# Which partial sums ScalarE copies out of PSUM, the order of six product chains, and the last store of a fused attention and FFN kernel

## Chip, core and metric

The kernel runs on one core of a Trainium2 chip. The metric is the time of one execution in microseconds (us) of device time. TensorE (PE) does the matmuls and loads their weights (PEld), VectorE (DVE) does elementwise work and scans, ScalarE (ACT) does copies and activations, GpSimd (POOL) masks, and SyncE (SP) issues every DMA.

## What is computed

A gated linear attention (batch 4, 8 heads, 768 steps, head size 48) is followed by a multiplicative feed-forward network on 3072 tokens of width 384:

```python
for t in range(S):
    state = f[:, :, t, :, None] * state + np.einsum('bhd,bhe->bhde', k[:, :, t], v[:, :, t])
    y[:, :, t] = np.einsum('bhd,bhde->bhe', q[:, :, t], state)
...
a = x @ w1
b = x @ w2
h = a * b @ w3
return (h @ w_out).astype(np.float32)
```

Everything is fp32. `w3 @ w_out` is folded into one 1024x384 matrix `wc` on the chip, so that the FFN is two "up" products (384 to 1024), their elementwise product, and one "down" product (1024 to 384).

## The kernel before, in words

The tokens go in six blocks of 512 (`ffn(n)`, n = 0 to 5). Attention runs in 24 units of 128 tokens and has ended by about 265 us; what follows is FFN work alone. Block 0 is computed plainly (`part`), blocks 1 and 2 by a seven-product scheme (`seven`), and blocks 3 to 5 by a bilinear scheme with 20 products in place of 24 (`many`). The change is in `many` and in `down`.

`many(g)` runs twice per block (g = 0, 1), so six times in all. It forms 20 products. Product (a, b) multiplies the a-th input (three token quarters by two halves, and sums of them, `X_SUMS`) by the b-th weight (twelve blocks of `w12`, and sums of them, `W_SUMS`), for `w1` and `w2` at once: two matmuls of 128x256 into the two halves of one PSUM bank of 128x512 (L1114). The products are arranged in six chains (`CHAINS`). A chain lives in one bank: its first product opens the bank, each later one adds to what is there, so that the bank holds a running sum. Twelve sums (`Y_SUMS`, L1158, VectorE) combine the running sums, and eight elementwise products (L1170, or L1174 with L1177 for the one that is a bank alone) give the result `ab`.

A running sum is read in one of two ways. If it is in the set `kept` (L1113 to L1116), ScalarE copies it to SBUF (`keep_`, L1135), and the next product of the chain waits for that copy, since it overwrites the bank by adding to it. If not, VectorE reads the bank itself in the sum (L1158). Before, only the last running sum of a chain can be read directly, so that no product waits for such a read. Twelve of the twenty are copied.

PSUM has eight banks. Four are tiles of one bank each (`f0` to `f3`). The other four are the halves of two tiles of two banks, `pa` and `py`, which attention uses whole; after attention, `bank()` (L369) hands out their halves one by one.

The order of all work is decided when the program is built: each step is put into `Plan` with an engine, an assumed cost, what it needs, a priority and the bank or temporary it takes, and `Plan.order` lists the steps by the earliest assumed start. Each engine then runs its instructions strictly in that order, and waits on semaphores for data of the others. Beside the FFN, ScalarE carries a check of the value range of the raw weights (`ranges`, L1513 to L1521): for each of 34 pieces, SP loads 512 KB into one of two buffers and ScalarE makes two passes over it, L1517 and L1521. These stand between the copies in ScalarE's order.

`down(i)` (twice per block) computes 2x128 output rows by seven groups of four matmuls of 128x192 (L863: m1, m6, m2, m7, m5, m4, m3), with copies by ScalarE (k1 at L1231, c11 at L1244) and sums by VectorE (u2 at L1237, u3 at L1250, c22 at L1261, c21 at L1267, c12 at L1275). c11 writes columns 0 to 191 of the upper rows, c12 columns 192 to 383. SP stores each 128 rows by one DMA of 192 KB (L1280).

In the names of the profile, the weights of product (a, b) show as the home of W sum b: `w` for b below 12, floor for b = 12, q for 15, 17, 25 and 26, k for 18, 19, 20 and 30, f for 21 and 22, bwd for 31, Q for 32, and K for 28 and 33.

Of the kernel before, what the change touches and what calls it, by code (L numbers as in the profile page):

```python
# [45 lines left out]
P = 128  # L46
# [5 lines left out]
DM = H * D  # L52
# [12 lines left out]
DH = DM // 2  # L65
# [25 lines left out]
W_LATE = 30  # L91
W_SINCE = 0.0
W_STEP = 0.0
CHAINS = [
    [(3, 0), (4, 4), (4, 23)],
    [(0, 13), (1, 6), (1, 26)],
    [(5, 8), (9, 25), (6, 17), (10, 31)],
    [(8, 28)],
    [(11, 14), (12, 22), (3, 19)],
    [(7, 10), (16, 21), (14, 12), (15, 32), (17, 30), (0, 33)],  # L100
]
X_SUMS = [
    (1, '+', 2, 0), (2, '+', 0, 1), (2, '+', 5, 2), (1, '+', 8, 3), (9, '+', 4, 4), (0, '+', 8, 5),
# [7 lines left out]
]  # L111
Y_SUMS = [
    (10, '+', 11), (7, '-', 20), (21, '-', 5), (4, '+', 14), (20, '-', 8), (24, '-', 18),
    (6, '+', 1), (13, '-', 16), (12, '+', 2), (28, '-', 15), (12, '-', 17), (30, '-', 9),
]
Y_ENDS = [22, 19, 23, 25, 26, 27, 29, 31]
NWT = 15
NXT = 11
FLOOR = 2.0**-60
# [141 lines left out]
def ranged(ctx, tc, q, k, f_logit, v, w1, w2, w3, w_out, out, ident, w12, wc, left):  # L261

    nc = tc.nc
# [70 lines left out]
    plan = Plan()  # L334
# [95 lines left out]
    def moves(n, size, rate, emit, deps, prio, late=0.0, since=0.0, lanes=("lane",)):  # L430


        for j in range(n):
            i = plan.add("SP", 0.45, (lambda: None) if j else emit, [d] if j else deps, prio - j * 1e-3, takes=lanes, lag=0.85, since=since)
            d = i
            t = plan.add("DMA", size / n / rate, lambda: None, [i], prio - j * 1e-3, lag=1.1 + late, frees=[i])
        return t
# [419 lines left out]
    stores, upq, downq, w_nodes, opened = [], [], [], [], []  # L857
# [10 lines left out]
    def ffn(n):  # L868
# [203 lines left out]
        def many_sums():  # L1072
            for k, (i, o, j, h) in enumerate(W_SUMS if not w_nodes else []):
                def emit(i=i, o=o, j=j, k=k):
                    nc.vector.tensor_tensor(w_view(4 * KM + k), w_view(i), w_view(j), op(o))
                w_nodes.append(plan.add("DVE", 0.69, emit, [over] + w_nodes[-1:], 100 * MANY + W_LATE + k, since=W_SINCE + W_STEP * k))
            old = [q[nm] for m in (n - 1, n - 2) for q in blk[m].get("seven", []) for nm in ("m5", "m6", "m7", "m4", "m3")]
# [8 lines left out]
        def many(g):  # L1086

            if ("X", 0) not in s:
                many_sums()
            n0 = 100 * n + 50 + 4 * g  # L1090
            np_ = sum(len(c) for c in CHAINS)
            uses = {}
            for i, _, j in Y_SUMS:
                for x in (i, j):
                    uses[x] = uses.get(x, 0) + 1
            task, bank_of, where_, hold, readers = {}, {}, {}, {}, {}
            ends_of = {}
            t = 0
            for c in CHAINS:
                ends_of[t + len(c) - 1] = True  # L1100
                t += len(c)
            kept = set()
            for i, _, j in Y_SUMS:
                direct = [x for x in (i, j) if x in ends_of and uses[x] == 1 and x not in Y_ENDS]
                kept |= {x for x in (i, j) if x < np_ and x not in direct[-1:]} if len(direct) < 2 else {min(direct)}
            begin = takes_ab(column(0, g), plan.add("PE", 0.0, lambda: None, x_task(0) + opened[-1:], n0))

            def product(t, c, first, a, b):
                def emit():
                    if first:  # L1110
                        banks[g, c] = bank()
                    for which in range(2):
                        lhs = up_weights(w12, which, b // 4, column(b % 4, g)) if b < 4 * KM else w_view(b)[:, which, g]  # L1113
                        nc.tensor.matmul(  # L1114
                            banks[g, c][:, which * TH : which * TH + TH], lhsT=lhs, rhs=x_node(a),
                            start=first and which == 0, stop=True, skip_group_check=True,  # L1116
                        )
                return emit

            banks = {}  # L1120
            t = 0
            for c, chain in enumerate(CHAINS):
                last = None
                for m, (a, b) in enumerate(chain):
                    deps = [begin] + x_task(a) + ([w_nodes[b - 4 * KM]] if b >= 4 * KM else []) + ([last] if m else opened[-1:])
                    task[t] = last = plan.add("PE", 0.86, product(t, c, m == 0, a, b), deps, n0 + 0.1 * c - 0.01 * m, takes=["f"] if m == 0 else [])
                    s["up"].append(last)
                    if m == 0:
                        opener = last
                        opened.append(last)  # L1130
                    bank_of[t] = (c, opener)
                    if t in kept:
                        def keep_(t=t, c=c):
                            where_[t] = temporary(plan.got)
                            nc.scalar.copy(where_[t], banks[g, c])  # L1135
                        last = plan.add("ACT", 0.57, keep_, [last], n0 - 200, takes=["t"], frees=[opener] if t in ends_of else [])
                        task[t] = hold[t] = last
                    t += 1
            left_ = dict(uses)
            for k, (i, o, j) in enumerate(Y_SUMS):  # L1140
                r = np_ + k
                deps = [task[i], task[j]]
                frees, mine = [], None
                for x in (i, j):
                    left_[x] -= 1
                    if x in hold and not left_[x] and x not in Y_ENDS:
                        deps += readers.get(x, [])
                        if mine is None:
                            mine = x
                        else:  # L1150
                            frees.append(hold[x])
                    elif x not in hold:
                        frees.append(bank_of[x][1])

                def emit(i=i, o=o, j=j, r=r, mine=mine):
                    x, y = (where_[v] if v in where_ else banks[g, bank_of[v][0]] for v in (i, j))
                    where_[r] = temporary(plan.got) if mine is None else where_[mine]
                    nc.vector.tensor_tensor(where_[r], x, y, op(o))  # L1158

                task[r] = plan.add("DVE", 0.69, emit, deps, n0 - 200, takes=["t"] if mine is None else [], frees=frees)  # L1160
                hold[r] = task[r] if mine is None else hold[mine]
                for x in (i, j):
                    readers.setdefault(x, []).append(task[r])
            for e, r in enumerate(Y_ENDS):
                def target(e=e):
                    return a_b(column(e % 4, g))[:, e // 4 * TH : e // 4 * TH + TH]

                if r in hold:
                    def emit(r=r, target=target):
                        nc.vector.tensor_tensor(target(), where_[r][:, 0:TH], where_[r][:, TH:TB], ALU.mult)  # L1170
                    done = plan.add("DVE", 0.43, emit, [task[r]] + readers.get(r, []), n0 - 200, frees=[hold[r]])
                else:
                    def half(r=r, target=target):
                        nc.scalar.copy(target(), banks[g, bank_of[r][0]][:, 0:TH])  # L1174
                    h = plan.add("ACT", 0.38, half, [task[r], begin], n0 - 200)
                    def emit(r=r, target=target):
                        nc.vector.tensor_tensor(target(), banks[g, bank_of[r][0]][:, TH:TB], target(), ALU.mult)  # L1177
                    done = plan.add("DVE", 0.43, emit, [h], n0 - 200, frees=[bank_of[r][1]])
                s["done"][g].append(done)
            s.setdefault("many", []).extend(task.values())  # L1180
# [13 lines left out]
        def down(i):  # L1194
            q = {}
            downq.append(q)
            final = n == NB - 1 and i == UB // 2 - 1
# [76 lines left out]
            def c12():  # L1274
                nc.vector.tensor_tensor(q["o1"][:, DH:DM], q["Z"], dns["u2"], ALU.add)  # L1275

            def store(half):
                def emit():
                    t0 = n * TB + (i + half * UB // 2) * P
                    nc.sync.dma_start(out[t0 : t0 + P], q["o1" if half == 0 else "o2"])  # L1280
                return emit

            n0 = 100 * n + 90 + i + 60 * (n > 1) + 30 * (n == NB - 2)
# [28 lines left out]
            pe("m3", m3, [q["c22"], q["S3"], q["m4"]] + ([judged] if final else []), -4)  # L1312
            dve("c12", 0.36, c12, [q["m3"], q["c11"]], frees=[q["m5"]])
            for half, deps in ((1, ("c21", "c22")), (0, ("c11", "c12"))):
                stores.append(moves(1, 197, 300, store(half), [q[nm] for nm in deps], -10))
            return q

        for i in range(UB // 2):
            q = down(i)
# [274 lines left out]
    first, last = {}, {}  # L1594
    for item in EARLY:
        if item in "ABCD":
            half, which = divmod("ABCD".index(item), 2)
            mine = pieces[which, half]
            first[item], last[item] = [j["deps"][0] for j in mine], mine
        else:  # L1600
            t = tk[int(item)]
# [389 lines left out]
```

## Time and profile before

| | us |
|---|---|
| median of 3 runs (465.94 to 467.49) | 466.26 |
| the profiled execution | 466.62 |
| its span | 464.9 |
| ScalarE busy, whole span | 206.8 |
| VectorE busy, whole span | 364.9 |
| first product of `many` starts on PE | 275.36 |
| end of the last instruction on VectorE (c12 of the last `down`) | 460.31 |

The profiled execution took 1.7 us more than its span, which runs from its first to its last instruction. Times in the text are from the span's start. A row of the timeline merges equal neighbours: "x4" at L1114 is one product, because each fp32 matmul is recorded as two. The length of a PE row includes the pipeline's depth, so that two rows that follow without a gap overlap; how far apart their starts are is what tells of a stall. The text in brackets at the end of a row is the idle time of the engine before it and the engine and line that ended it.

### The profile page before, as it was taken

The page shows a single profiled execution, that of the slowest core. Times are in us where ns is not written, and L with a number is a line of the kernel's source. Part 1 is how long each engine was busy: PE and PEld are TensorE (multiplying, and loading weights), DVE is VectorE, ACT ScalarE, POOL GpSimd, SP SyncE. Part 2 cuts the span into 40 slices and gives each one's busy share as a digit, 9 for nine tenths or more (in the row PEclk, how much of TensorE's full clock was granted, in tenths as well). Part 3 has the DMA queues.
Part 4 walks back from the last instruction along what each step waited for, and adds up shares of the span by engine and source line. Part 5 has one row for each costly group of instructions (what it writes and reads, how often), then busy time and mean ns, then how long its engine had stood idle before and what let it go on. Part 6 is the DMA issues. An engine that isn't in the chain of part 4 may idle for free.

```text
span 464.9 us, 11763 instructions
## 1 busy us (share of the span) xinstructions
PE 454.4 (98%) x4800; PEld 396.0 (85%) x4800; DVE 364.9 (78%) x657; ACT 206.8 (44%) x468; POOL 64.6 (14%) x90
## 2 busy tenths in 40 slices
PE   8989999999999999999999999999999999999995
PEld 7778886666899888889998889998899977889995
DVE  8988999999898998989973599894687366867451
ACT  4565344532224444443332456565764567642000
POOL 9330001121122332322331000000000000000000
PEclk9999999999999999999999999999999999999999
DMA  6899898733346664545423336534364433100111
GB/s 180 263 307 282 276 347 276 261 96 93 83 111 191 200 181 122 140 134 165 106 64 107 120 124 204 170 129 151 119 202 159 151 122 94 45 1 0 35 68 39
DMA packets 43165, 68.75 MB, mean 148 GB/s; under 512 B 5201, under 2 KB 28242, under 8 KB 42082
## 3 DMA queue, kind: packets, MB, share of 16 engines
q1 hardware_dynamic: 43106, 67.95, 47.5%
q8 instruction: 39, 0.64, 0.6%
q14 instruction: 20, 0.16, 0.1%
HBM read 58.88 MB, written 9.04 MB: 146 GB/s over the span
## 4 chain that ended last, share of the span: by engine, by line
PE 94%; POOL 2%; DVE 1%; issue 1%; ACT 0%; POOLq 0%; DVEq 0%
PE f L863 25%; PE f L959 14%; PE f L1114 12%; PE f L1446 9%; PE pa L1114 5%; PE py L1114 5%; PE py L863 5%; PE pa L863 3%; PE py L619 3%; PE pa L545 2%; PE pa L652 2%; PE f L559 2%; PE py L638 2%; PE pa L959 1%; POOL ab L403 1%; PE f L365 1%
## 5 line engine op out<-in xcount | busy, mean ns | idle before, releaser
L675 POOL TENSOR_SCALAR_AFFINE_SELECT A<-A 64x512 f32<-64x512 f32 (+1 forms) x46 | 43.4, 943 | 104.5 <-ACT A L669 102.3
L1446 PE MATMUL f<-place 128*128 128x384 f32 x128 | 42.7, 488 | 0.0
L863 PE MATMUL f<-xt,w 128*128 128x256 f32 x192 | 42.1, 380 | 0.0
L863 PEld LDWEIGHTS f<-xt,w 128*128 128x128 f32 x192 | 36.3, 190 | 5.0
L1446 PEld LDWEIGHTS f<-place 128*128 128x128 f32 x128 | 23.8, 190 | 15.3
L959 PE MATMUL f<-xt,w 128*128 128x256 f32 x132 | 34.2, 379 | 0.0
L863 PE MATMUL f<-place 128*128 128x192 f32 x184 | 33.9, 329 | 0.0
L514 DVE TENSOR_TENSOR_SCAN bwd<-gate,back 112x512 f32<-112x512 f32 x24 | 30.9, 1285 | 0.7
L492 DVE TENSOR_TENSOR_SCAN fwd<-gate,floor 112x512 f32<-112x512 f32 x24 | 30.5, 1271 | 1.1 <-ACT gate L484 0.2
L863 PEld LDWEIGHTS f<-place 128*128 128x128 f32 x184 | 30.1, 190 | 0.8 <-DVE place L1237 0.3
L959 PEld LDWEIGHTS f<-xt,w 128*128 128x128 f32 x132 | 24.8, 190 | 3.1
L1521 ACT ACTIVATE A<-A,back 128x512 f32<-128x512 f32 x34 | 26.6, 781 | 0.5
L811 ACT ACTIVATE ys<-py 112x512 f32<-112x512 f32 x22 | 13.1, 595 | 28.2 <-PE py L638 27.3
L1384 ACT ACTIVATE place<-place 128x512 f32<-128x512 uint32 (+2 forms) x24 | 21.1, 890 | 9.9 <-DMA place<-in_w_dram 7.6
L1517 ACT ACTIVATE A<-A 128x512 f32<-128x512 f32 x34 | 23.3, 685 | 4.0 <-DMA A<-in_w_dram 4.0
L863 PE MATMUL f<-wc,ab 128*128 128x192 f32 x128 | 23.4, 326 | 0.0
L959 PE MATMUL f<-place 128*128 128x256 f32 x84 | 22.4, 385 | 0.0
L775 POOL TENSOR_TENSOR G<-lasts,gate 112x4 f32<-112x4 f32 x20 | 10.7, 533 | 81.3 <-ACT lasts L497 50.0
L863 PEld LDWEIGHTS f<-wc,ab 128*128 128x128 f32 x128 | 21.3, 190 | 0.3
L484 ACT ACTIVATE gate<-f 112x512 f32<-112x512 f32 x22 | 13.9, 632 | 15.8 <-DMA f<-in_f_logit_dram 5.6
L619 PEld LDWEIGHTS py<-A,vt 64*64 64x64 f32 (+1 forms) x672 | 13.3, 127 | 7.3 <-issue 5.7
L619 PE MATMUL py<-A,vt 64*64 64x64 f32 (+1 forms) x672 | 18.1, 223 | 0.2
(343 smaller groups left out, 1041.5 us busy)
## 6 DMA issues: line engine op xcount, KB each, us to landing
A<-in_w_dram SPq DMA_DIRECT2D x28, 512.0 KB, 3.9
place<-in_w_dram SPq DMA_DIRECT2D x8, 1024.0 KB, 6.7
place<-in_w_dram SPq DMA_DIRECT2D x12, 512.0 KB, 7.5
out_dram<-o SPq DMA_DIRECT2D x24, 192.0 KB, 1.9
q<-in_q_dram SPq DMA_DIRECT2D x46, 96.0 KB, 2.9
vt<-in_v_dram SPq DMA_DIRECT2D x23, 192.0 KB, 3.2
k<-in_k_dram SPq DMA_DIRECT2D x44, 96.0 KB, 2.6
yt<-ys SPq DMA_DIRECT2D x44, 96.0 KB, 2.7
```

The costliest lines, as they stand in the source:

```text
L484: nc.scalar.activation(gate[u % 2][:, 0:NQ], fu, AF.Sigmoid)
L492: nc.vector.tensor_tensor_scan(s["P"], gate[u % 2][:, 0:NQ], floor, 0.0, ALU.mult, ALU.max)
L514: nc.vector.tensor_tensor_scan(s["R"][:, ::-1], gate[u % 2][:, NQ:0:-1], back[:, ::-1], 0.0, ALU.mult, ALU.max)
L619: done = nc.tensor.matmul(y_block(u, hp, par, half)[p0 : p0 + w], lhsT=s["v"][half * W : half * W + W, h * D : h * D + w], rhs=s["A"][half ...
L675: nc.gpsimd.affine_select(out=a, in_=a, pattern=pattern, compare_op=ALU.is_ge, fill=0.0, base=0, channel_multiplier=-1,)
L863: nc.tensor.matmul(out_, lhsT=lhs[i], rhs=rhs[i], start=start and i == 0, stop=i == len(lhs) - 1, skip_group_check=True,)
L959: nc.tensor.matmul(q[nm][:, which * TH : which * TH + TH], lhsT=lhs[i](which), rhs=rhs[i], start=start and which == 0 and i == 0, stop=i = ...
L1114: nc.tensor.matmul(banks[g, c][:, which * TH : which * TH + TH], lhsT=lhs, rhs=x_node(a), start=first and which == 0, stop=True, skip_grou ...
L1384: nc.scalar.activation(lo.bitcast(F32), lo, AF.Copy, bias=2.0, scale=2.0**-51)
L1446: nc.tensor.matmul(w3s["p", jc], lhsT=w3s[jc][:, kc * P : kc * P + P], rhs=wos[:, kc], start=(kc == 0), stop=(kc == KF - 1),)
L1517: return lambda: nc.scalar.activation(a, a, AF.Abs, accum_out=sums_[:, i : i + 1])
L1521: return lambda: nc.scalar.activation(a, a, AF.Sign, bias=small, accum_out=counts[:, i : i + 1])
```

## The change

```diff
+SLACK_M = 0.0
+DIRECT = 1
 CHAINS = [
     [(3, 0), (4, 4), (4, 23)],
+    [(5, 8), (9, 25), (6, 17), (10, 31)],
     [(0, 13), (1, 6), (1, 26)],
-    [(5, 8), (9, 25), (6, 17), (10, 31)],
+    [(7, 10), (16, 21), (14, 12), (15, 32), (17, 30), (0, 33)],
+    [(11, 14), (12, 22), (3, 19)],
     [(8, 28)],
-    [(11, 14), (12, 22), (3, 19)],
-    [(7, 10), (16, 21), (14, 12), (15, 32), (17, 30), (0, 33)],
 ]
...
-            for i, _, j in Y_SUMS:
-                direct = [x for x in (i, j) if x in ends_of and uses[x] == 1 and x not in Y_ENDS]
-                kept |= {x for x in (i, j) if x < np_ and x not in direct[-1:]} if len(direct) < 2 else {min(direct)}
+            latest = {i: i for i in range(np_)}
+            for k, (i, _, j) in enumerate(Y_SUMS):
+                late_, other = (i, j) if latest[i] > latest[j] else (j, i)
+                latest[np_ + k] = latest[late_]
+                alone = late_ < np_ and uses[late_] == 1 and late_ not in Y_ENDS and (late_ in ends_of or DIRECT)
+                kept |= {x for x in (i, j) if x < np_ and not (x == late_ and alone)}
...
-                    elif x not in hold:
+                    elif x not in hold and x in ends_of:
                         frees.append(bank_of[x][1])
...
                 task[r] = plan.add("DVE", 0.69, emit, deps, n0 - 200, takes=["t"] if mine is None else [], frees=frees)
+                for x in (i, j):
+                    if x < np_ and x not in hold and x not in ends_of:
+                        made[x + 1]["deps"].append(task[r])
...
-            def store(half):
+            def store(half, c0=0, c1=DM):
                 def emit():
                     t0 = n * TB + (i + half * UB // 2) * P
-                    nc.sync.dma_start(out[t0 : t0 + P], q["o1" if half == 0 else "o2"])
+                    nc.sync.dma_start(out[t0 : t0 + P, c0:c1], q["o1" if half == 0 else "o2"][:, c0:c1])
...
             for half, deps in ((1, ("c21", "c22")), (0, ("c11", "c12"))):
+                if final and half == 0:
+                    stores.append(moves(1, 98, 300, store(0, 0, DH), [q["c11"]], -10))
+                    stores.append(moves(1, 98, 300, store(0, DH, DM), [q["c12"]], -10))
+                    continue
```

`Y_SUMS` and `Y_ENDS` are renumbered to the new order of the products; the sums are the same twelve. The new rule for `kept` looks at each sum of two running sums and takes the one whose product comes later in the list: if it is used once, VectorE reads it from the bank, whether or not its chain goes on; the other one, and any that is used more than once, is copied. Where the chain goes on, its next product waits for the VectorE sum in place of a copy (`made[x + 1]`).

Read directly before: (8,28), (1,26), (3,19), (4,23) and (10,31), each the end of its chain. Read directly after: (8,28) and (3,19), which end their chains, and (5,8) and (7,10), which open theirs. So (5,8) and (7,10) lose their copy, and (4,23), (1,26) and (10,31) gain one: thirteen copies per call of `many` in place of twelve. The product (9,25) now waits for the sum (5,8)+(4,4), and (16,21) for the sum (1,6)+(7,10).

The second edit stores the last 128 rows to be finished in two DMAs of 96 KB, the first after c11, the second after c12.

In the built program PE has as many instructions as before and the same matmuls, in another order from 278 us on; VectorE has the same count; ScalarE has six copies more; SP has one DMA more.

More of the change, by code (lines that the diff above doesn't have):

```diff
@@ L112 @@
 Y_SUMS = [
-    (10, '+', 11), (7, '-', 20), (21, '-', 5), (4, '+', 14), (20, '-', 8), (24, '-', 18),
-    (6, '+', 1), (13, '-', 16), (12, '+', 2), (28, '-', 15), (12, '-', 17), (30, '-', 9),
+    (19, '+', 16), (4, '-', 20), (21, '-', 9), (8, '+', 10), (20, '-', 5), (24, '-', 14),
+    (3, '+', 1), (18, '-', 12), (17, '+', 2), (28, '-', 11), (17, '-', 13), (30, '-', 6),
 ]
-Y_ENDS = [22, 19, 23, 25, 26, 27, 29, 31]
+Y_ENDS = [22, 15, 23, 25, 26, 27, 29, 31]
 NWT = 15
@@ L1095, in many @@
                     uses[x] = uses.get(x, 0) + 1
-            task, bank_of, where_, hold, readers = {}, {}, {}, {}, {}
+            task, made, bank_of, where_, hold, readers = {}, {}, {}, {}, {}, {}
             ends_of = {}
@@ L1125, in many @@
                     deps = [begin] + x_task(a) + ([w_nodes[b - 4 * KM]] if b >= 4 * KM else []) + ([last] if m else opened[-1:])
-                    task[t] = last = plan.add("PE", 0.86, product(t, c, m == 0, a, b), deps, n0 + 0.1 * c - 0.01 * m, takes=["f"] if m == 0 else [])
+                    made[t] = task[t] = last = plan.add("PE", 0.86, product(t, c, m == 0, a, b), deps, n0 + 0.1 * c - 0.01 * m, takes=["f"] if m == 0 else [], slack=SLACK_M)
                     s["up"].append(last)
```

## Prediction

> **What bounds the kernel now.** I read the page's shares first, then the chain of work that ended last, then the windows of the stage that the change touches, then the timeline at the places where PE stood still.
>
> ```profile
> span 464.9 us, 11763 instructions
> ...
> PE 94%; POOL 2%; DVE 1%; issue 1%; ACT 0%; POOLq 0%; DVEq 0%
> ```
>
> The chain is PE for 94% of the span. The change moves no matmul off PE, so it can gain or lose only where PE stands still, and behind PE's end. The windows by stage (columns: window, its length, busy us of PE, PEld, DVE, ACT, POOL, then clock, DMA share, GB/s):
>
> ```profile
> 264.00:330.00 66.00, 66.00 (x335) 60.10 (x334) 54.05 (x107) 40.02 (x98) 0.00 (x0) 1.00 0.47 151
> 330.00:400.00 70.00, 68.39 (x342) 61.20 (x341) 44.90 (x88) 44.44 (x105) 0.00 (x0) 1.00 0.45 143
> 400.00:460.00 60.00, 59.91 (x332) 56.51 (x330) 35.73 (x83) 14.58 (x31) 0.00 (x0) 1.00 0.06 21
> ```
>
> PE is idle 1.6 us in 330 to 400 and nearly never elsewhere; ScalarE has 25 us or more to spare in each window, VectorE 12 or more. So their load does not count, only how late single copies and sums are. The larger of the two stops, from the timeline:
>
> ```profile
> 370.81 1.89 PE L1114 MATMUL pa<-xt,w 128*128 128x256 f32 x8
> ...
> 372.54 1.03 PE L1114 MATMUL f<-place,k 128*128 128x256 f32 x4
> ...
> 372.74 0.58 ACT L1135 COPY Q<-pa 128x512 f32<-128x512 f32 x1 [1.14 <-PE pa L1114]
> ...
> 373.22 0.66 ACT L1517 ACTIVATE A<-A 128x512 f32<-128x512 f32 x1
> ...
> 373.87 0.57 ACT L1135 COPY ys<-pa 128x512 f32<-128x512 f32 x1
> ...
> 374.50 1.13 PE L1114 MATMUL pa<-xt,q 128*128 128x256 f32 x4 [0.93 <-ACT ys L1135]
> ```
>
> A product takes 0.86 us of PE (two in pa from 370.81, next row at 372.54). The next row after 372.54 should begin at 373.40 and begins at 374.50: 1.10 lost, and its second product comes 0.10 late as well (375.46, 0.96 after the first), since a product that waited has its weight load exposed. The cause is worth reading: the first of the two products into pa had ended at 371.67, ScalarE stood idle 1.14, yet copied it only at 372.74, 0.20 after the second had ended. **The two halves of pa are waited for as one tile**, though `Plan` counts them as two banks. The same is seen at py at 384.94. Adding up the starts of PE's rows from 264 us on gives the stage's whole loss: 1.10 + 0.84 (384.94) + 0.13 (403.38), 0.10 behind each, 0.24 at 359.2, and two of 0.08, in all **2.8 us**. That is the most that a better order could gain here.
>
> **The change, part by part.**
>
> *Six more copies on ScalarE.* 6 x 0.58 = 3.5 us on an engine idle for 25 us and more in each window: nothing by load, only by lateness, counted below. If that cover were gone, 3.5 us.
>
> *Sums that read PSUM.* Twelve sums as before, four with a PSUM operand in place of five, all of one length in this trace:
>
> ```profile
> 371.63 0.69 DVE L1158 TENSOR_TENSOR place<-place,Q 128x512 f32<-128x512 f32 x1 [1.17 <-ACT Q L1135]
> ...
> 372.35 0.69 DVE L1158 TENSOR_TENSOR place<-place,py 128x512 f32<-128x512 f32 x1
> ```
>
> The first reads SBUF twice, the second PSUM: 0.69 both, so I cost it at nothing. [...]
>
> *The new order.* I went through the changed kernel's order of instructions from 278 us on, engine by engine, and at each place where PE waits for ScalarE or VectorE set the PE work in between against the time until release, with these durations from before: product 0.86; group of four at L863 1.30; PE's end to a copy 0.20; copy 0.58, the next may start 0.47 after; copy or sum to the next engine 0.05; L1521 0.76 from start to start; copy of 192 columns 0.32; sum 0.69, the next starts 0.60 after, or 0.72 if it needs the first; elementwise product 0.42, the next 0.33 after. Done on the old order, the same working gives the stops at 374.5, 384.9 and 403.4 and no other over 0.05, within 0.03 us of what the trace has. On the new order those three are gone and others come, all of them in pa or py:
>
> - Product (17,30) into half of pa, about 308, in block 3: before it stand m1 of a `down` into the other half, then m6 (1.30). From m1's end: a copy at 0.20 (that of (15,32), held back by m1 in the same tile), L1521 at 0.67, k1 at 1.43 to 1.75, PE at 1.80 against 1.30. **0.5**.
> - m7 of that `down`, about 313: from m2's end PE has 1.30 + 0.86 = 2.16. The copy of (17,30) (held back by m2) 0.20 to 0.78, a sum 0.83 to 1.52, two elementwise products from 1.55 and 1.88, u2 at 2.21 to 2.57, PE at 2.62. **0.46**.
> - Product (3,19), about 333: one product (0.86) stands between (8,28) in the other half of pa and it. Copy of (12,22), held back by (8,28), 0.20 to 0.78; a sum at 0.83; the sum that reads (8,28) from the bank at 1.43 to 2.12; PE at 2.17. It waits for that read only because the halves are one tile. **1.31**.
> - Product (6,17), about 419: two copies out of pa in a row, 0.20 and 0.67 to 1.25, PE at 1.30 against 0.86. **0.44**.
> - Three small ones: 0.14 at 352, where (16,21) waits for its sum, 0.13 at 370, 0.06 at 429.
>
> With 0.10 behind each of the seven and two tight places like those that cost 0.08 before: 2.71 + 0.33 + 0.7 + 0.16 = 3.9. Against 2.8: **1.1 us more**. The other waits of (9,25) and (16,21) for a sum have 0.8 to 2.4 us to spare, as two or more products stand between.
>
> *The last store.* c12 is the last row of the timeline, and the page lists the DMA issues by line (KB of each, us from issue to landing):
>
> ```profile
> 459.95 0.36 DVE L1275 TENSOR_TENSOR o<-f,place 128x192 f32<-128x192 f32 x1 [0.94 <-PE f L863]
> ```
>
> ```profile
> out_dram<-o SPq DMA_DIRECT2D x24, 192.0 KB, 1.9
> ...
> yt<-ys SPq DMA_DIRECT2D x44, 96.0 KB, 2.7
> ```
>
> SP issues the store at 460.37, its first packet runs 0.8 us later, and eight packets of 1,536 B follow on each DMA engine at 0.066 us, 0.53 in all; SP's wait ends at 463.37. Rows of half the length take away between nothing and all of that 0.53; the nearest 96 KB row, yt, lands in 2.7 against 1.9, amid other traffic and with shorter rows, which bounds a loss at 0.8. I take half of 0.53, rounded down: -0.2. The extra first store comes after c11 (455.06 before), where SP issues nothing until 459.03: hidden; without that cover one issue, 0.34. Instruction packets of 16 KB run beside the last store (460.63, 1.36 us), and hold two engines until 462.87: this may eat the gain. [...]
>
> *Sum.* +1.1 - 0.2 = +0.9. The profiled execution had 466.62 (span 464.9 and 1.7 around it): 467.5. The runs' median is 466.26, 0.36 below it: 467.2. I forecast **467.4**, 0.2% more. About 0.3% (1.4 us) is what a measurement of this kernel can tell from no change.
>
> **Rivals.**
>
> *The old stops go and no new ones come* (the readings above are late by chance of my sums, or the halves are not waited for as one in these places). For it: three stops do go, and VectorE's direct reads spare two copies on PE's way. Against: the working finds every stop of before. Then -2.8 - 0.2: 463.6. Faster.
>
> *ScalarE's queue makes the copies late: slower.* Place: the copies of (4,23), (1,26) and (10,31) and the copies behind them, between passes L1517 and L1521 that wait for their loads (ScalarE waits about 4 us for them now, at no cost to PE). Price: a copy behind one such pass more costs 0.76, and there are 18 added copies less 12 removed. From two such places on beyond what I counted, 1.1 + 1.5 - 0.2 = 2.4 over: 469.0. Equally, if hand-offs last 0.05 longer, I get 1.6 for 1.1. Against: most copies have 0.3 us and more to spare.
>
> *The store's split loses*: 0.8 for -0.2 gives 468.4.
>
> **Chances.** The forecast and its neighbours within 0.3%: 0.63. Faster rival: 0.09. ScalarE's queue 0.2 and the store 0.08, both slower. The range leaves out the faster rival and the tail beyond 469.2: 465.3 to 469.2. The forecast is near the bound to slower, 467.66.
>
> **What would show it.** In the profile after: no stop of PE at 372.7 and 384.3; stops of 0.4 to 1.4 at about 308, 313, 333 and 419, on pa or py; PE idle of some 3 us between 264 and 460; c12's end at about 461.2; (9,25) and (16,21) without a wait above 0.2. It is wrong if PE's waits name L1517, or sums at (9,25), or if the last store's landing moves by over 0.5.

## The result and the profile after

The changed kernel takes 467.17 us (median of 22 runs, 466.21 to 471.23), the kernel before 465.93 us (22 runs, 465.01 to 468.21): a ratio of 1.0026, with a 95% interval of 1.0014 to 1.0039. So it is slower by 0.3%, or by 0.7 to 1.8 us. The forecast was 467.4 and 0.2% more. The profiled execution took 467.24.

The page and the windows of the kernel after (columns as before; line numbers have moved: L1163 is the sum that was L1158, L1140 the copy that was L1135, L865 was L863, L1529 and L1533 were L1517 and L1521):

```profile
span 465.4 us, 11779 instructions
...
PE 93%; DVE 2%; ACT 1%; SPq 1%; issue 1%; DMA 1%; POOL 1%; POOLq 0%; DVEq 0%
```

```profile
264.00:330.00 66.00, 65.35 (x330) 59.13 (x329) 50.91 (x101) 40.40 (x97) 0.00 (x0) 1.00 0.46 151
330.00:400.00 70.00, 68.76 (x345) 61.62 (x344) 47.07 (x93) 45.54 (x107) 0.00 (x0) 1.00 0.46 143
400.00:461.00 61.00, 60.70 (x335) 56.97 (x333) 35.34 (x81) 16.71 (x37) 0.00 (x0) 1.00 0.07 22
```

PE is now idle in all three windows, 0.65 + 1.24 + 0.30 us, where before it was idle almost only in the second. ScalarE and VectorE still have time to spare everywhere. The largest stop, from the timeline of the kernel after:

```profile
329.22 1.03 PE L1119 MATMUL pa<-place,f 128*128 128x256 f32 x4
...
330.08 1.03 PE L1119 MATMUL pa<-place,K 128*128 128x256 f32 x4
...
330.94 1.03 PE L1119 MATMUL f<-place,Q 128*128 128x256 f32 x4
331.14 0.59 ACT L1140 COPY ys<-pa 128x512 f32<-128x512 f32 x1 [1.14 <-PE pa L1119]
...
331.76 0.69 DVE L1163 TENSOR_TENSOR a<-ys,a 128x512 f32<-128x512 f32 x1 [6.31 <-ACT ys L1140]
...
332.37 0.69 DVE L1163 TENSOR_TENSOR ys<-pa,ys 128x512 f32<-128x512 f32 x1
332.37 0.66 ACT L1529 ACTIVATE A<-A 128x512 f32<-128x512 f32 x1
...
332.93 0.19 ACT L1529 ACTIVATION_READ_ACCUMULATOR A<-A 128x1 f32 x1
...
333.20 1.10 PE L1119 MATMUL pa<-xt,k 128*128 128x256 f32 x4 [1.23 <-ACT A L1529]
```

The last row is (3,19) in one half of pa. It should begin 0.86 after 330.94, at 331.80, and begins at 333.20: 1.40 lost. (12,22) had ended at 330.08, but its copy began only at 331.14, 0.20 after (8,28) had ended in the other half. VectorE's read of that other half ended at 333.06, and PE went on. The bracket names ScalarE's L1529, which ended at 333.12; the built program has PE wait for the VectorE sum and for the copy of (12,22), which had ended at 331.73, and not for that pass. L1529 is the old L1517, and the prediction had called itself wrong if PE's waits name L1517: by the letter that sign is there. A releaser named by a profile is a guess from times; the run with single tiles below (after_halves), where (3,19) starts before the same pass has ended, settles it.

All seven stops stand where they were forecast. From the starts of PE's rows:

| product after the stop | forecast, us | measured, us |
|---|---|---|
| (17,30), about 308 | 0.50 | 0.51 |
| m7 of the `down`, about 313 | 0.46 | 0.46 |
| (3,19), about 333 | 1.31 | 1.40 |
| (16,21), about 352 | 0.14 | 0.17 |
| a `down` group, about 370 | 0.13 | 0.14 |
| (6,17), about 419 | 0.44 | 0.46 |
| a `down` group, about 429 | 0.06 | 0.14 |
| behind the seven | 0.7 | 0.67 |
| two tight places | 0.16 | 0.16 |
| sum | 3.9 | 4.1 |

Before, the sum was 2.8. The difference is 1.3 us, and it is what c12's end shows against the first product of `many`: 184.94 us from one to the other before, 186.26 after. Behind c12, the span goes on for 3.86 us, in place of 4.58:

```profile
460.29 1.85 SPq L1288 DMA_DIRECT2D out_dram<-o  x2
461.20 0.36 DVE L1283 TENSOR_TENSOR o<-f,place 128x192 f32<-128x192 f32 x1 [0.94 <-PE f L865]
```

### The profile page after: what moved, and what is told of

Its sections match the earlier page's. It is cut to its first block, busy times and chain, and to the rows that moved or that the text cites. A ratio compares the mean times of both kernels' runs of the same rounds, so it can differ in the third digit from the quotient of the medians.

```text
span 465.4 us, 11779 instructions
## 1 busy us (share of the span) xinstructions
PE 455.5 (98%) x4800; PEld 396.2 (85%) x4800; DVE 363.7 (78%) x657; ACT 210.6 (45%) x474; POOL 64.8 (14%) x90
## 4 chain that ended last, share of the span: by engine, by line
PE 93%; DVE 2%; ACT 1%; SPq 1%; issue 1%; DMA 1%; POOL 1%; POOLq 0%; DVEq 0%
PE f L865 24%; PE f L961 14%; PE f L1119 11%; PE f L1458 9%; PE py L1119 6%; PE pa L1119 5%; PE pa L865 5%; PE py L865 4%; PE py L621 3%; PE pa L547 2%; PE pa L654 2%; PE f L561 2%; PE py L640 2%; PE pa L961 1%; PE f L367 1%; PE py L961 1%
## 5 line engine op out<-in xcount | busy, mean ns | idle before, releaser
L865 PE MATMUL f<-xt,w 128*128 128x256 f32 x192 | 42.1, 380 | 0.0
L865 PEld LDWEIGHTS f<-xt,w 128*128 128x128 f32 x192 | 36.3, 190 | 5.0
L1458 PEld LDWEIGHTS f<-place 128*128 128x128 f32 x128 | 23.8, 190 | 15.3
L865 PE MATMUL f<-place 128*128 128x192 f32 x192 | 35.1, 328 | 0.0
L865 PEld LDWEIGHTS f<-place 128*128 128x128 f32 x192 | 31.4, 190 | 0.4 <-issue 0.2
L1533 ACT ACTIVATE A<-A,back 128x512 f32<-128x512 f32 x34 | 26.4, 775 | 0.5
L1529 ACT ACTIVATE A<-A 128x512 f32<-128x512 f32 x34 | 23.3, 686 | 2.9 <-DMA A<-in_w_dram 2.9
L865 PE MATMUL f<-wc,ab 128*128 128x192 f32 x112 | 20.5, 326 | 0.0
L865 PEld LDWEIGHTS f<-wc,ab 128*128 128x128 f32 x112 | 18.7, 190 | 0.3
```

The costliest lines, as they stand in the source:

```text
L865: nc.tensor.matmul(out_, lhsT=lhs[i], rhs=rhs[i], start=start and i == 0, stop=i == len(lhs) - 1, skip_group_check=True,)
L1458: nc.tensor.matmul(w3s["p", jc], lhsT=w3s[jc][:, kc * P : kc * P + P], rhs=wos[:, kc], start=(kc == 0), stop=(kc == KF - 1),)
L1529: return lambda: nc.scalar.activation(a, a, AF.Abs, accum_out=sums_[:, i : i + 1])
L1533: return lambda: nc.scalar.activation(a, a, AF.Sign, bias=small, accum_out=counts[:, i : i + 1])
```

## Experiments

Theory: PE stops because the halves of pa and py, two banks each, are one tile to the program's waits; a new order meets this in other places, and the change's loss is the difference of two such chances. Rivals: the reads in the middle of chains or the added copies are late by themselves; the split store costs (or gains) the difference.

**The chains alone (chains_only).** The changed kernel with the last store whole:

```diff
-                if final and half == 0:
-                    stores.append(moves(1, 98, 300, store(0, 0, DH), [q["c11"]], -10))
-                    stores.append(moves(1, 98, 300, store(0, DH, DM), [q["c12"]], -10))
-                    continue
```

> The new chains and the new rule for copies, with the last store whole as before. Theory (PE's stops at waits for a half of pa or py make the difference, the split store next to nothing): the seven stops of the changed kernel at 308, 313, 333, 352, 370, 419 and 429 us come again, 4.1 us in all against 2.8 before, c12 ends at about 461.5, and the time is 1.1 to 1.5 us over before (ratio 1.0024 to 1.0032). Rival 1 (the split store is what costs): within 0.3 us of before. Rival 2 (the split store saves the 0.7 us by which the profile's tail behind c12 is shorter after): 1.9 to 2.1 us over before.

Measured: 467.13 us against 466.20 of before, 0.93 over by the medians; ratio 1.0010, 0.9996 to 1.0024 (the ratios of this section are those on record, and not quotients of the medians). In its profile all seven stops are there with the same lengths to 0.01 us, and from the first product to c12 pass 186.25 us. The ratio is below what the theory expected, and reaches only its lower end. It settles neither rival by itself; the profile shows that the stops belong to the chains and not to the store.

**The store alone (store_only).** The kernel before with the second edit alone (the `store` function and the branch above, added).

> The kernel before with the last store in two column parts, chains as before. Theory: PE's order is the old one, with its stops at 372.7 and 384.3; the last packets are half as long, which saves 0.1 to 0.3 us behind c12: 0 to 0.3 us under before. Rival 1 (the split costs, two completions in place of one): 0.5 us or more over before. Rival 2 (the whole 0.7 us of the shorter tail is the split's): 0.6 to 0.8 us under before.

Measured: 465.56 against 466.20, ratio 0.9977, 0.9961 to 0.9993: 0.64 us under, more than the theory allowed, and the size of rival 2. PE's loss from 264 us on is the old 2.8, and first product to c12 184.93. In its profile the tail behind c12 is 4.11 us in place of 4.58; but the first product, too, came 0.5 earlier than in the profile before (274.88), in a stage that the edit doesn't touch, so that this pair alone doesn't tell how much of the 0.64 is the split's. All profiles together say more, below.

**Halves as tiles of their own, old chains (before_halves).** When `bank()` first hands out a half after attention, the pool of pa and py is closed and four tiles of one bank are opened in its place. The order of instructions on every engine stays the same.

```diff
+    first_ps = ExitStack()
+    ps = first_ps.enter_context(tc.tile_pool(name="ps", bufs=1, space=PSUM))
...
-            nm = ("pa", "py")[(plan.got - NF) // 2]
-            if nm not in found:
-                found[nm] = ps.tile([P, 2, NQ], F32, name=nm)
-            return found[nm][:, plan.got % 2]
+            if "ps_h" not in found:
+                first_ps.close()
+                found["ps_h"] = ctx.enter_context(tc.tile_pool(name="ps_h", bufs=1, space=PSUM))
+            return found["ps_h"].tile([P, NQ], F32, name=f"h{plan.got - NF}")
```

> The kernel before, in which the four PSUM banks that the halves of pa and py occupy become four tiles of one bank each once attention is over; the planned order of work is the same. Theory (readers and writers of one half are made to wait for the other, because the two are one tile): the stops at 372.7 and 384.3 go, PE loses under 0.5 us from 264 us on in place of 2.8, and the time is 2.2 to 2.8 us under before (ratio 0.994 to 0.9955). Rival (the copies themselves are late, behind the passes L1517 and L1521 in ScalarE's queue): both stops stay at half their size or more, and the gain is under 1.0 us.

Measured: 463.25 us against 466.20, 2.95 under by the medians; ratio 0.9939, 0.9920 to 0.9959. The place where the kernel before stood still for 1.10 us, in the timeline of this one:

```profile
370.48 1.89 PE L1115 MATMUL h<-xt,w 128*128 128x256 f32 x8
...
371.54 0.59 ACT L1136 COPY Q<-h 128x512 f32<-128x512 f32 x1 [0.28 <-PE h L1115]
...
372.03 0.69 ACT L1518 ACTIVATE A<-A 128x512 f32<-128x512 f32 x1
...
372.69 0.58 ACT L1136 COPY ys<-h 128x512 f32<-128x512 f32 x1
```

The two products start at 370.48 and 371.34. The first copy begins at 371.54, 0.20 after its own product, and no longer after the second. So the pass L1518 and the second copy behind it are done a product earlier. No stop is left from 264 us on, and from the first product to c12 pass 182.14 us, 2.8 less than before: the whole loss. The rival (copies late by themselves) falls.

**Halves as tiles of their own, new chains (after_halves).** The same edit on the changed kernel.

> The changed kernel with the same four single tiles in place of the halves, planned order unchanged. Theory: all seven stops go, the one at 333 (1.4 us) too, since the product (3,19) no longer waits for VectorE's read of the other half; PE loses under 0.5 us in place of 4.1, the time is 3.3 to 4.1 us under the changed kernel and so within 0.4 us of before's chains with single tiles: the change itself is worth nothing either way, and its loss is how its order meets the shared tiles. Rival (VectorE's reads in the middle of chains and the six more copies are late by themselves): the stops at 333, 352 and 419 stay, and the kernel remains 1 us or more slower than before's chains with single tiles.

Measured: 463.29 us, ratio to before 0.9924, 0.9900 to 0.9948. From the first product to c12 again 182.14. The place of the largest stop, in this kernel's timeline:

```profile
328.27 1.03 PE L1120 MATMUL h<-place,f 128*128 128x256 f32 x4
...
329.13 1.03 PE L1120 MATMUL h<-place,K 128*128 128x256 f32 x4
329.33 0.58 ACT L1141 COPY ys<-h 128x512 f32<-128x512 f32 x1 [0.28 <-PE h L1120]
...
330.56 0.68 DVE L1164 TENSOR_TENSOR ys<-h,ys 128x512 f32<-128x512 f32 x1
330.58 0.68 ACT L1530 ACTIVATE A<-A 128x512 f32<-128x512 f32 x1
...
330.86 1.03 PE L1120 MATMUL h<-xt,k 128*128 128x256 f32 x4
331.15 0.18 ACT L1530 ACTIVATION_READ_ACCUMULATOR A<-A 128x1 f32 x1
```

(3,19) begins at 330.86, while VectorE still reads the other bank (330.56 to 331.24). The same sum in the same place of the order, and PE doesn't wait for it, nor for the pass (here L1530), which ends at 331.33. With single tiles the two kernels are equal, 463.25 and 463.29 (the first with the whole last store, the second with the split one), and the stage from the first product to c12 is 182.14 in both: the chains and the rule for copies are worth nothing in themselves, and the reads in the middle of chains, before (9,25) and (16,21), don't hold PE up there. That rival falls too.

**One of the two tiles split (after_pa_single).** The changed kernel with pa's halves as single tiles and py as it was:

```diff
...
+            if plan.got >= NF + 2:
+                if "py" not in found:
+                    found["py"] = ps_y.tile([P, 2, NQ], F32, name="py")
+                return found["py"][:, plan.got % 2]
...
```

> The changed kernel with the two halves of pa as single tiles once attention is over, py still one tile. Theory: four of the seven stops are in pa (308, 333, 370, 419) and go; the one at 313 is in py, but comes from a copy out of pa that m2 held back, and goes too; the small ones in py at 352 and 429 stay, 0.2 us with 0.1 behind each. PE loses about 0.4 us in place of 4.1: 3.3 to 3.8 us under the changed kernel, within 0.5 us of the version with four single tiles. Rival (any change of the banks moves the order of work and removes the stops by luck): no such split by tile; stops of 0.4 us and more remain or new ones come in pa.

Measured: 463.13 us (4 runs), ratio to before 0.9947, 0.9928 to 0.9966. By the medians that is 4.0 under the changed kernel, more than expected; by the stage from the first product to c12 it is 3.63, inside what was expected. Two stops remain, both in py, before (16,21) (0.17) and at the last one of the list (0.14), with 0.10 and 0.08 behind them; first product to c12 182.63, 0.49 more than with four single tiles. The windows show almost nothing of it, because a product's row lasts 1.03 us and the next one begins 0.86 after it, so that the recorded idle time is 0.17 short of a stop: 0.01 us in the second, and the 0.45 of the last lie behind PE's end at 456.55.

```profile
264.00:330.00 66.00, 66.00 (x335) 60.29 (x334) 51.20 (x102) 41.71 (x99) 0.00 (x0) 1.00 0.45 147
330.00:400.00 70.00, 69.99 (x353) 63.46 (x352) 46.92 (x94) 47.38 (x111) 0.00 (x0) 1.00 0.45 143
400.00:457.00 57.00, 56.55 (x317) 53.63 (x315) 34.69 (x81) 13.25 (x29) 0.00 (x0) 1.00 0.08 27
```

The stop at 313 was in py and went with pa, as the working had it: there m7 waited for u2, which stood on VectorE behind a sum whose copy m2 had held back in pa.

**No reads in the middle of chains (after_direct0).** The changed kernel with `DIRECT = 0`. In this kernel a copy of block 3 overwrites the buffer u2 before block 2's last elementwise products have read it, so that part of block 2's result is formed from other data; its instructions, sizes and waits are as described.

> The changed kernel with DIRECT = 0: only ends of chains are read directly, so (5,8) and (7,10) are copied again and 15 running sums per call are copied; halves shared as in the changed kernel. Theory (stops are where an order happens to meet the shared tiles, not what direct reads cost): other stops of like size, by the working of the prediction in pa at about 373 (0.87), 421 (0.83), 423 (0.2), 448 and 450 (0.6 each, in the last downs), 3.6 us in all with what follows them: within 0.6 us of the changed kernel, 0.4 to 1.4 us over before. Rival (the reads in the middle of chains are the loss): the stops go, and it is as fast as before or faster by up to 2 us.

Measured: 466.78 us, ratio to before 1.0021, 1.0010 to 1.0032; 0.4 us under the changed kernel by the medians, 0.21 by the stage from the first product to c12. Five stops, in pa, four of them in PE's list of waits:

```profile
PE pa L1119 <- ACT ab L1182: 0.7, 1, 0.7
PE pa L1119 <- ACT ys L1140: 0.7, 1, 0.7
PE pa L865 <- DVE place L1258: 0.4, 1, 0.4
PE pa L865 <- DVE o L1269: 0.4, 1, 0.4
```

(This view, too, counts the recorded idle time.) By the starts of rows they are 0.90 at 372, 0.84 at 420, 0.20 at 422, and 0.61 each at 447 and 449, against 0.87, 0.83, 0.2, 0.6 and 0.6 by the working; 3.9 in all with what stands behind them. A third order, without the reads that the change introduced and with two copies more per call, loses about as much in other places. That its stops go with single tiles as well was not run.

**The split with single tiles (before_halves_store, after_halves_store0).** The first is before_halves with the split store, the second after_halves with the whole one.

> The kernel before with four single tiles and with the last store in two column parts: the fastest combination by what was measured so far. Theory (the split saves 0.2 to 0.6 us behind c12, as it did alone): 462.6 to 463.1, 3.0 to 3.4 us under before; 0.2 to 0.6 us under the same kernel with the whole store. Rival (the split is worth nothing): 463.2 to 463.4.

> The changed kernel's chains with four single tiles and the last store whole. With no stops left in either order, this and the chains of before with the split store differ by the split alone. Theory: no stop of PE from 264 us on, 0.2 to 0.6 us slower than the chains of before with single tiles and the split store. Rival (the split is worth nothing): equal within 0.2 us. If the chains themselves cost anything without the shared tiles, this is slower than 463.6.

Measured: 462.92 us (ratio 0.9947, 0.9927 to 0.9966) and 463.07 us (0.9940, 0.9922 to 0.9958): 0.15 apart by the medians, which is what the second rival said (within 0.2) and less than the theory's 0.2 to 0.6; by the ratios the kernel with the whole store is even the faster one. The intervals are over 1.6 us wide, so the times decide neither. 462.92 is the lowest median of all, 0.7% under before by the medians and 0.5% by the ratio, with after_halves_store0, after_halves, after_pa_single and before_halves within 0.4 us of it.

All ten profiles together tell the parts apart (us; the tail is the span less c12's end):

| kernel | span's start to first product | first product to c12 | tail | store |
|---|---|---|---|---|
| before | 275.36 | 184.94 | 4.58 | whole |
| after | 275.30 | 186.26 | 3.86 | split |
| chains_only | 276.67 | 186.25 | 4.25 | whole |
| store_only | 274.88 | 184.93 | 4.11 | split |
| before_halves | 275.37 | 182.14 | 4.28 | whole |
| after_halves | 275.53 | 182.14 | 4.11 | split |
| after_pa_single | 274.31 | 182.63 | 3.85 | split |
| after_direct0 | 274.57 | 186.05 | 4.08 | split |
| before_halves_store | 275.04 | 182.14 | 4.07 | split |
| after_halves_store0 | 275.30 | 182.14 | 4.38 | whole |

The middle column repeats to 0.01 us for the same chains and tiles. The tail is 4.25 to 4.58 (mean 4.37) with the whole store, 3.85 to 4.11 (mean 4.01) with the split: **0.36 us gained**. The four pairs that differ in the store alone gain 0.47 (before), 0.39, 0.27 and 0.21. The longest tail, that of before, has a packet of instructions beside the store that the others have not (last section); without it the mean of the whole stores is 4.30 and the gain 0.29. The rest of the scatter between these ten executions is in the first column, 274.3 to 276.7, in a stage that no edit was aimed at.

## Why the prediction was right, point by point

*PE bounds, and only its stops count.* Right. The change is 1.3 us of stops more and 0.36 of tail less, 0.96 together; the measured medians differ by 1.24 with an interval from 0.7 to 1.8.

*The two halves are waited for as one tile.* Right, and shown: with single tiles and the same order the stops go from 2.8 and 4.1 us to nothing. The bound "2.8 us is the most that a better order could gain" is met by the single tiles without any better order.

*The order laid against the durations of before.* Right in all seven places of the new order (but for the reason of the one at 352, below), with terms 0.2 too small in sum: 333 had 0.09 more than the working, 429 0.08 more. These are the two stops where PE waits for two engines at once. There an instruction of PE's queue, 0.05 us long (at 333.10 and 429.62), waits for VectorE ahead of the weight load, which itself waits for ScalarE; from VectorE's end to PE's start pass 0.15 us, where 0.05 to 0.06 pass from the end of the one engine waited for at the other five, and the working took 0.05 for all. One place of the old order the working did not find, though it says that it found every stop: at 359.46 PE stood 0.13 us for u2 (L1237, 359.06 to 359.41). The prediction has that loss in its 2.8 and not in its list of stops.

*Six more copies cost nothing by load; a sum that reads PSUM costs as much as one that reads SBUF.* Right: ScalarE's busy time went from 206.8 to 210.6 us, and both sums in the timeline of 333 take 0.69, the first from SBUF, the second from pa.

*The waits of (9,25) and (16,21) have time to spare.* Right, and more so than the prediction had it. It puts the stop at 352 to (16,21) waiting for its sum; that sum, (1,6)+(7,10), had ended at 342.87. What PE waited for was c22 of a `down` (L1269, 351.62 to 351.98), which reads the other half of py:

```profile
PEld py L1119 <- DVE o L1269: 0.4, 1, 0.4
```

So this stop, too, is one of the shared tile; its length (0.14 forecast, 0.17 measured) was near, its reason was not.

*The last store: -0.2.* The sign was right and the size a little small: 0.36 over ten profiles, 0.29 without the one of before. The packets of the last store took 0.038 us each with 768 B and 0.067 with 1,536 B (medians), so that eight of them save 0.23: half of the 0.53 was a fair term. What makes the rest is open; the pairs scatter by 0.26. Between the two profiles of before and after, though, SP's wait for the last store ends 2.37 us after its issue in place of 3.00, a move of more than the 0.5 that the prediction named as a sign that it is wrong. By the ten profiles about half of these 0.63 is the split's; the rest goes with the long tail of before.

*Sum.* 467.5 by the profiled execution and 467.2 by the median; measured 467.24 and 467.17. That the median is met to 0.03 is in part luck: the sum had a rise of 0.9, the medians show 1.24, and the kernel before came out 0.33 lower in 22 runs (465.93) than in the three that the forecast started from (466.26).

*Rivals.* The faster one fell: three stops went and seven came. ScalarE's queue was not what made copies late, as after_halves shows, and the store's split gained.

## What to carry to other kernels

Here the planner counted banks and the program waited by tiles, without a sign in the source; a copy that began 0.20 us after somebody else's product, with its engine idle for 1.14 (372.74 before, 331.14 after), is how the timeline told it. Before changing an order to remove stops, look at what the waiter waits for: here the tiles' shape was worth 2.8 us in one order and 4.1 in another, and three orders of nearly the same work differed by 1.3. Where one engine bounds, such stops can be worked out beforehand from the order of instructions and a dozen durations (here the seven to 0.09 us each); where times scatter, cut the profile at points that an edit cannot move.

## What the runs showed of the hardware

- The FFN stage repeats to 0.01 us in 182 from profile to profile when chains and tiles are the same, while the first 275 us vary by 2.4. Kernels of this kind are best compared by stage.
- ScalarE's copies of 128x512 take 0.58 us but start 0.48 apart, and two VectorE sums 0.69 but 0.61 apart, or 0.72 when the second needs the first: the time to the next engine and the time to the next instruction are two numbers.
- Where PE had to wait, the second recorded matmul behind the stop is late as well, by 0.07 to 0.10 us at all seven stops of the changed kernel: each stop costs that on top. The weight load of the first begins there 0.00 to 0.03 us ahead of its matmul, that of the second 0.16 (L865) or 0.21 (L1119) ahead, as in rows without a stop.
- At the stops of the changed kernel where PE waited for one engine, its matmul began 0.05 to 0.06 us after that engine's end (five stops); where it waited for two, 0.15 (two stops).
- Packets of instructions run near the last store in all ten profiles: two of 16 KB (0.9 to 1.4 us each) and two of 8 KB (0.3 to 0.7). In the profile of before a 16 KB packet began 0.32 us after c12 and ran beside the store, whose last packet ended 2.56 us after c12, and its tail is the longest, 4.58; in the other three profiles with the whole store the last packet ended 2.13 to 2.29 after c12. In those, and in the six with the split store, one 16 KB packet began 0.4 to 1.0 us ahead of c12 and the next behind the store's last packet. That is one observation.
